# A fused attention and two-MLP kernel on one core: places for activations in the first MLP's blocks, the pace of the second weights' conversions, and places for the last splits

## The chip, the cores and the metric

The kernel runs on one core of one Trainium2 chip. The metric is device time in microseconds (us), the median of several runs. Before the change it is 1630.62 us, the median of 3 runs (1630.06 to 1632.49).

## The reference

```python
def _attn_ref(q, k, v, g_norm):            # 8 batches, 8 heads, 576 tokens, 64 wide
    kv = np.einsum('bhsd,bhse->bhde', k, v)
    out = np.einsum('bhsd,bhde->bhse', q, kv)
    rms = np.sqrt(np.mean(out * out, axis=-1, keepdims=True) + 1e-06)
    return out / rms * g_norm
def _moe_ref(x, w_in, w_out, s, b):        # x 4608 x 512, w_in 512 x 2048, w_out 2048 x 512
    r = np.maximum(x @ w_in, 0.0)
    return (s * (r * r) + b) @ w_out
def _moe2_ref(x, w_in, w_out):
    h = x @ w_in
    return (h * np.cos(h)) @ w_out
# reference: attention, then x as 4608 x 512, then _moe_ref, then _moe2_ref, all float32;
# the weights arrive as float64
```

## The kernel before, in words

The work has three stages. **Stage A** does the attention and the first MLP for three blocks of 512 tokens. **Stage B** does the first MLP for the other tokens, in four blocks of 768, as 32 pairs (a pair is two of the sixteen 128-wide slices of the 2048 hidden columns; 90 matmuls). **Stage C** does the second MLP for all tokens, in six blocks of 768, as 48 pairs. Stages B and C form the first matmul of a pair from seven products of sums of quarters (`mm_h2`, line 966, matmuls at L981); each product leaves a bank of PSUM by a copy on ACT, the "snap" (L994), or by a sum on DVE (L1001 in stage B, L1003 in stage C). The second matmul is `mm_o1` in stage B (L875) and seven "units" per pair in stage C (`mm_unit`, L1092), three at once and four stored ones, which are worked off a block later. Fp32 operands go to the PE as an upper and a lower part: the upper is a cast on ACT, the lower a subtraction on DVE (L1203 and L1204 in stage B, in `act1_pair`; L1029 and L1030 in stage C, in `split_form`).

During stage B the weights of the second MLP are also made ready (`w_conv`): a load of 512 KB into the single place `raw` (L388, L392), then ACT (L405, L415) and DVE (L406 to L423), then sums and splits (`w_sums`, `o_sums`, `split_store`; L456, L458, L477, L504) whose parts go to DRAM (`w2i_d`, `w2n_d`, `w2s_d`; L467, L495). The five places `t0` to `t4` hold both those parts, until their store has landed, and the snaps.

The order of the work on every engine is not written by hand: `Plan.run` simulates all engines with the costs given to `op`, and issues each operation when its model would start it; among those ready, the one with the earliest `due`. Each engine then works in that order, and waits on the chip for what is really late. A DMA is assumed to land `LANDS` = 0.5 us after its transfer. Buffers are named places; an operation takes the place that comes free first in the model. The places that matter:

```python
RING, PLACES, X_RAW = WI[:6], slots("s", 11), LATE[:4]   # weights of stage B; raw x
RING2, O_RING, ACTS2 = WI[:5], WI[5:9], WI[9:]           # stage C: weights, activations
NOW, STORED = [*SPLIT_F[3:], *RAW], SPLIT_F[:3]          # splits of units
ACTS1 = WI[6:]                                           # activations of stage B
```

`WI` has sixteen places `wi0` to `wi15`. In stage B a pair takes six of `ACTS1`: two for h, two for upper and two for lower parts. At the very end `block_out` works off 32 stored units of the last block (four sums `y0` to `y3`, the loop over p, of eight units each); between them DVE adds each finished sum to what is kept (L1136).

Of the kernel before, what the change touches and what calls it, by code (L numbers as in the profile page):

```python
# [12 lines left out]
F32R = mybir.dt.float32r  # L13
# [9 lines left out]
TB2 = 768  # L23
# [22 lines left out]
NOW_AT = tuple(UNIT_STEP * i for i in (2, 5, 8))  # L46
STORED_AT = 10 * UNIT_STEP
FIRST_LOADS = {0: -39.5, 1: -38.5, 2: -36.5, 3: -36.3}
WARM = 24
# [22 lines left out]
class Plan:  # L72
# [18 lines left out]

    def op(self, eng, cost, due, fn, w=(), p=(), r=(), keep=(), after=()):

        o = Op()
        o.eng, o.cost, o.due, o.fn, o.refs = eng, cost, due, fn, list(dict.fromkeys([*w, *p, *r, *keep]))
        deps = set(after)
        for x in r:
            deps.update(x.writers)  # L100
        for x in w:
            deps.update(x.writers)
            deps.update(x.readers)
        for x in p:
            deps.update(x.readers)
        for x in r:
            x.readers.append(o)
        for x in w:
            x.writers, x.readers = [o], []
        for x in p:  # L110
            x.writers.append(o)
        deps.discard(o)
        o.wait, o.users, o.ready = len(deps), [], 0.0
        for d in deps:
            d.users.append(o)
        for x in o.refs:
            x.left += 1
        self.ops.append(o)
        return o

    def run(self):
# [31 lines left out]
        while n < len(self.ops):  # L153
# [13 lines left out]
            if o.eng in self.ISSUE:  # L167
                engines[o.eng] = t + self.ISSUE[o.eng]
                dma = max(dma, t + self.TO_DMA) + o.cost * self.BUSY
                end = seen = dma + self.LANDS  # L170
                lanes[o.eng].pop(0)
                lanes[o.eng].append(end)
            else:
                end = engines[o.eng] = t + o.cost * self.SLACK[o.eng]
                seen = end + self.AFTER[o.eng]
# [20 lines left out]
def fused_kernel(  # L196
# [126 lines left out]

    RING, PLACES, X_RAW = WI[:6], slots("s", 11), LATE[:4]
    RING2, O_RING, ACTS2 = WI[:5], WI[5:9], WI[9:]
# [5 lines left out]
    ACTS = PARTS = [*WI[6:], *RAW]  # L331
    ACTS1 = WI[6:]
    SNAP = [*T, *C]
# [44 lines left out]
    def w_conv(ph, kind, f, by, load_by=None, after=()):  # L378
# [23 lines left out]

        op("SP", 1.45 if kind == "i" else 1.35, by - 12 if load_by is None else load_by, load, w=[raw], after=after)

# [47 lines left out]
    def split_store(t, n, by, ref, to, start=0):  # L452
# [9 lines left out]
        for z, part in enumerate((hi, lo)):  # L462
# [5 lines left out]

            op("SP", n * 0.0013, by, store, p=[ref], r=[part])

    def o_sums(u, tu, tv, by):
# [19 lines left out]
        for t, parts in ((ya, ((now[:, 2], w2n_ref[u]), stored(2))), (yb, (stored(1), stored(3)))):  # L491
            both = split_store(t, 512, by, None, None)
            for z, part in enumerate(both):
                for n, (d, ref) in enumerate(parts):
                    op("SP", 0.335, by, lambda z=z, part=part, n=n, d=d: nc.sync.dma_start(  # L495
                        out=d[:, z, :], in_=f32(part.t[:, n * HB:(n + 1) * HB])), p=[ref], r=[part])

# [619 lines left out]
    def block_out(j):  # L1117
# [32 lines left out]
        for p in range(4):  # L1150
            name = f"y{p}" if end else "y"
            for u in range(NU):
# [3 lines left out]
                f = stored_f[n0 + u][p]  # L1156
                x = split_form(STORED, lambda f=f: f.t, f, at - 3)
                after = []
# [36 lines left out]
    def act1_pair(n, h):  # L1195

        g = {}
        for f, by in ((1, pair_due(n + 1)), (0, pair_due(n + 1) + 2)):
            x, hi, lo = h[f], *(sref(ACTS1, F32R, (TB2,)) for z in range(2))
            op("ACT", 0.75, by, lambda x=x: nc.scalar.activation(x.t, x.t, AF.Square), w=[x])  # L1200
# [3 lines left out]
            op("DVE", 0.88, by + 5, lambda x=x, hi=hi, lo=lo: nc.vector.tensor_tensor(  # L1204
                out=lo.t, in0=x.t, in1=f32(hi.t), op=ALU.subtract), w=[lo], r=[x, hi])
            g[f] = lambda z, hi=hi, lo=lo: (hi, lo)[z].t, [hi, lo]
# [59 lines left out]
    for n in range(NPAIR):  # L1266
# [8 lines left out]
        while n and n < NP1 and done_convs < 4 * NU and (  # L1275
                done_convs - EARLY_CONVS) * (NP1 - 10) <= (n - 1) * (4 * NU - EARLY_CONVS):
            conv2(pair_due(n + 1) + 24, [done[n - 1]])
# [50 lines left out]
```

## Time and profile before

| | |
|---|---|
| median of 3 runs | 1630.62 us |
| the profiled execution, its own time | 1630.51 us |
| its span, first to last instruction | 1628.7 us |
| PE busy | 1596.6 us (98%), 11248 matmuls |
| DVE busy / ACT busy | 1150.5 us (71%) / 1124.9 us (69%) |
| DMA | 383.71 MB, mean 236 GB/s |

The profiled execution takes 1.8 us outside its span. Stage A runs to about 361 us, stage B to about 899 us, stage C to the end. The engines work side by side, so the time is set by PE, which has nearly all the work, and by what PE waits for.

### The profile page before, as it was taken

To read this page: it belongs to the slowest core of one execution; us is meant where nothing else is said; L and a number is where in the kernel's file an instruction comes from. 1 tells how busy PE (TensorE), PEld (TensorE's weight loads), DVE (VectorE), ACT (ScalarE), POOL (GpSimd) and SP (SyncE) were. 2 spreads that over 40 slices of the span, in tenths; PEclk is the share of its full clock that TensorE was granted. 3 is DMA by queue.
4 is the path that set the end of the run, shared out by engine and by line. 5 is a ranking of instruction groups with operands and counts; after the bars stand their busy time and mean duration, and the time that the engine had idled before them with its cause. 6 is when DMAs were issued, how large, how long until landed. Compare 5 with 4: busy or idle time off the path is not lost.

```text
span 1628.7 us, 30373 instructions
## 1 busy us (share of the span) xinstructions
PE 1596.6 (98%) x11248; PEld 1468.8 (90%) x11248; DVE 1150.5 (71%) x2194; ACT 1124.9 (69%) x2013; POOL 54.5 (3%) x90
## 2 busy tenths in 40 slices
PE   8999999999999999999999899999999999999998
PEld 7668888889898998899999889999999999999997
DVE  6887775674655665657323798887888888888775
ACT  5865543446576676667545898788788788788773
POOL 0011222100000000000000000000000000000000
PEclk9999999999999999999999999999999999999999
DMA  9746878847678878878644777878878878878866
GB/s 317 224 105 170 219 194 202 259 120 234 219 235 278 281 232 267 280 231 267 200 130 135 224 236 232 303 245 269 302 237 267 306 249 272 298 256 258 270 205 196
DMA packets 240180, 383.71 MB, mean 236 GB/s; under 512 B 86432, under 2 KB 152480, under 8 KB 240032
## 3 DMA queue, kind: packets, MB, share of 16 engines
q1 hardware_dynamic: 233440, 360.20, 70.2%
q0 software_dynamic: 6016, 20.45, 4.6%
q8 instruction: 89, 1.46, 0.4%
q10 hardware_dynamic: 576, 1.11, 0.2%
q14 instruction: 59, 0.48, 0.1%
HBM read 312.48 MB, written 69.21 MB: 234 GB/s over the span
## 4 chain that ended last, share of the span: by engine, by line
PE 87%; DMA 5%; ACT 4%; DVE 3%; issue 1%; SPq 0%; POOL 0%; DVEq 0%; ACTq 0%; POOLq 0%
PE banks L981 31%; PE banks L1092 20%; PE banks L875 13%; PE banks L827 6%; PE banks L774 3%; PE banks L775 3%; PE banks L776 3%; PE banks L823 3%; PE banks L600 1%; PE banks L694 1%; DMA raw<-in_moe_w_in_dram 1%; PE banks L732 1%; DMA w2i_d<-t 1%; DMA w2n_d<-t 1%; DMA w2s_d<-t 1%
## 5 line engine op out<-in xcount | busy, mean ns | idle before, releaser
L981 PE MATMUL banks<-shared,wi 128*128 128x384 f32 x2232 | 455.7, 338 | 9.8 <-ACT t L994 7.1
L981 PEld LDWEIGHTS banks<-shared,wi 128*128 128x128 f32 x2232 | 388.0, 188 | 19.1 <-ACT t L994 10.5
L1092 PE MATMUL banks<-wi,fs 128*128 128x256 f32 x2376 | 309.0, 283 | 4.7 <-DVE fs L1030 3.0
L1092 PEld LDWEIGHTS banks<-wi,fs 128*128 128x128 f32 x2376 | 301.6, 190 | 6.9 <-DVE fs L1030 4.5
L875 PE MATMUL banks<-wi,wo 128*128 128x512 f32 (+1 forms) x1536 | 290.3, 337 | 3.0 <-DVE wi L1204 3.0
L875 PEld LDWEIGHTS banks<-wi,wo 128*128 128x128 f32 x1536 | 244.7, 188 | 34.0 <-DVE wi L1204 5.5
L994 ACT ACTIVATE t<-banks 128x384 f32<-128x384 f32 x214 | 104.1, 488 | 90.7 <-PE banks L981 67.3
L1030 DVE TENSOR_TENSOR fs<-fu,fs 128x384 fp32r<-128x384 f32 x216 | 116.4, 553 | 31.7 <-ACT fs L1029 30.6
L1029 ACT CAST fs<-fu 128x384 fp32r<-128x384 f32 x216 | 108.4, 507 | 35.2 <-PE banks L1092 34.9
L981 PE MATMUL banks<-late,wi 128*128 128x384 f32 x552 | 116.7, 338 | 2.1 <-DVE wi L1001 1.5
L981 PE MATMUL banks<-g,wi 128*128 128x384 f32 x504 | 113.4, 340 | 2.6 <-ACT t L994 1.6
L827 PE MATMUL banks<-g,wo 128*128 128x512 f32 x432 | 108.9, 395 | 0.0
L1204 DVE TENSOR_TENSOR wi<-wi,wi 128x768 fp32r<-128x768 f32 x64 | 59.6, 954 | 62.9 <-PE banks L875 61.8
L981 PEld LDWEIGHTS banks<-late,wi 128*128 128x128 f32 x552 | 95.3, 188 | 4.6 <-DVE wi L1001 2.1
L1049 DVE CUSTOM_DVE_ANT_0 wi<-wi,wi 128x768 f32<-128x768 f32 x96 | 91.3, 952 | 7.3 <-ACT wi L1047 7.0
L827 PEld LDWEIGHTS banks<-g,wo 128*128 128x128 f32 x432 | 79.7, 188 | 17.2
L1043 ACT ACTIVATE wi<-wi 128x768 f32<-128x768 f32 x96 | 80.2, 842 | 16.2 <-DVE wi L1003 14.6
L981 PEld LDWEIGHTS banks<-g,wi 128*128 128x128 f32 x504 | 85.6, 188 | 5.3 <-ACT t L994 2.8
L1092 PE MATMUL banks<-wi,raw 128*128 128x256 f32 x648 | 89.8, 283 | 0.4 <-DVE raw L1030 0.3
L1092 PEld LDWEIGHTS banks<-wi,raw 128*128 128x128 f32 x648 | 85.9, 189 | 1.4 <-DVE raw L1030 1.0
L774 PE MATMUL banks<-shared,wi 128*128 128x512 f32 x192 | 82.2, 428 | 1.9 <-ACT shared L751 1.6
L1045 ACT ACTIVATE wi<-wi 128x768 f32<-128x768 f32 x96 | 80.7, 841 | 2.7 <-PE banks L875 1.2
(171 smaller groups left out, 2439.8 us busy)
## 6 DMA issues: line engine op xcount, KB each, us to landing
wi<-w2i_d SPq DMA_DIRECT2D x144, 512.0 KB, 4.7
wi<-w1i_d SPq DMA_DIRECT2D x96, 512.0 KB, 4.8
wi<-w2s_d SPq DMA_DIRECT2D x96, 512.0 KB, 4.5
wi<-w2n_d SPq DMA_DIRECT2D x48, 512.0 KB, 4.3
late<-x_d SPq DMA_DIRECT2D x36, 384.0 KB, 6.5
w2i_d<-t SPq DMA_DIRECT2D x48, 256.0 KB, 4.4
wi<-w2n_d SPq DMA_DIRECT2D x48, 256.0 KB, 4.1
wi<-w2i_d SPq DMA_DIRECT2D x48, 256.0 KB, 4.5
```

Source lines behind the costliest of these rows:

```text
L774: nc.tensor.matmul(h.t, wh, hi, start=(c == 0), stop=False)
L827: nc.tensor.matmul(o.t, a[:, sl], b, start=(first and z == 0), stop=(last and z == 2))
L875: nc.tensor.matmul(dst, x[:, sl], y[:, src], start=(first and z == i == 0), stop=(last and z == 2), skip_group_check=a >= 4)
L981: nc.tensor.matmul(o.t[:, 0:HT], a, b, start=(first and c == z == 0), stop=(c == 1 and z == 2), skip_group_check=not first)
L994: op("ACT", 0.38, by + 1, lambda: nc.scalar.activation(dst(), o.t[:, 0:HT], func), p=[s], r=[o])
L1029: op("ACT", 0.42, by, lambda: nc.scalar.copy(x.t[:, 0], src()), w=[x], r=[ref], after=after)
L1030: op("DVE", 0.47, by + 0.4, lambda: nc.vector.tensor_tensor(out=x.t[:, 1], in0=src(), in1=f32(x.t[:, 0]), op=ALU.subtract), w=[x], r=[ref])
L1043: op("ACT", 0.75, by, lambda u=u, x=x: nc.scalar.activation(u.t, x.t, AF.Identity, scale=1.0 / TWO_PI, bias=0.25), w=[u], r=[x])
L1045: op("ACT", 0.75, by + 0.5, lambda u=u, v=v: nc.scalar.activation(v.t, u.t, AF.Identity, bias=MAGIC), w=[v], r=[u])
L1049: op("DVE", 0.88, by + 2, lambda u=u, v=v: nc.vector._custom_dve(TENSOR_ADD_SAT, out=u.t, in0=u.t, in1=v.t, s0=0.5 - 1.7e-7, s1=-0.5 + 1.7 ...
L1092: nc.tensor.matmul(dst, x.t[:, a, sl], w.t[:, at, b, :], stop=(last and z == 2), start=(first and z == 0 and (m == 0 or (m == 2 and opens) ...
L1204: op("DVE", 0.88, by + 5, lambda x=x, hi=hi, lo=lo: nc.vector.tensor_tensor(out=lo.t, in0=x.t, in1=f32(hi.t), op=ALU.subtract), w=[lo], r= ...
```

## The change

1. `op` gets a `lag`, which `run` adds to the time at which it assumes a DMA has landed: 2.5 us for the loads of the second weights (`w_conv` with ph = 1), 1.5 us for the stores of their parts (and for those of stage A that go through `split_store`).
2. The ring of stage B's weights has five places instead of six; the sixth, `wi5`, goes to the activations (eleven instead of ten).
3. The lower parts of stage B's activations may also lie in the four places of raw x (`LOWER`); they wait until those places exist (`after=over`).
4. The 32 conversions are spread over stage B to its 27th pair or so, instead of its 22nd (`NP1 - 5` for `NP1 - 10`).
5. In the last block the splits of the sums `y1` to `y3` may also lie in the seven places `ACTS2`, once the units done at once (a, b, c) are through.

```diff
+LOAD_LAG, STORE_LAG = 2.5, 1.5
...
-                end = seen = dma + self.LANDS
+                end = seen = dma + self.LANDS + o.lag
...
-    RING, PLACES, X_RAW = WI[:6], slots("s", 11), LATE[:4]
+    RING, PLACES, X_RAW = WI[:5], slots("s", 11), LATE[:4]
...
-    ACTS1 = WI[6:]
+    ACTS1 = WI[5:]
+    LOWER = [*ACTS1, *X_RAW]
...
-        op("SP", 1.45 if kind == "i" else 1.35, by - 12 if load_by is None else load_by, load, w=[raw], after=after)
+        op("SP", 1.45 if kind == "i" else 1.35, by - 12 if load_by is None else load_by, load, w=[raw], after=after,
+           lag=LOAD_LAG if ph else 0.0)
...
-            op("SP", n * 0.0013, by, store, p=[ref], r=[part])
+            op("SP", n * 0.0013, by, store, p=[ref], r=[part], lag=STORE_LAG)
...
-                x = split_form(STORED, lambda f=f: f.t, f, at - 3)
+                free = end and p
+                x = split_form([*STORED, *ACTS2] if free else STORED, lambda f=f: f.t, f, at - 3,
+                               [unit_ops[j, z, "last"] for z in "abc"] if free else ())
...
-            x, hi, lo = h[f], *(sref(ACTS1, F32R, (TB2,)) for z in range(2))
+            x, hi, lo = h[f], *(sref(s, F32R, (TB2,)) for s in (ACTS1, LOWER))
...
-                out=lo.t, in0=x.t, in1=f32(hi.t), op=ALU.subtract), w=[lo], r=[x, hi])
+                out=lo.t, in0=x.t, in1=f32(hi.t), op=ALU.subtract), w=[lo], r=[x, hi], after=over)
...
-                done_convs - EARLY_CONVS) * (NP1 - 10) <= (n - 1) * (4 * NU - EARLY_CONVS):
+                done_convs - EARLY_CONVS) * (NP1 - 5) <= (n - 1) * (4 * NU - EARLY_CONVS):
```

No operation is added or removed; what changes is places and, through the model, the order on each engine. Lines behind the edits have moved by one to six: L1204 becomes L1210, L1030 L1034, L1136 L1140. Three places show what moves.

DVE in stage B, two lower parts of the 17th pair (L1204; after the change L1210). A name is a place's kind and a running number; a row's brackets hold the engines it waits for. Before:

```order
L458 TENSOR_TENSOR t_7006<-c_6976,t_7005 128x512 [waits DMAHW5_49,DMAHW7_49,DMAHW2_49,Activation_49]
L1204 TENSOR_TENSOR wi_7034<-wi_6896,wi_6943 128x768 [waits PE_49]
L1204 TENSOR_TENSOR wi_7038<-wi_6818,wi_6991 128x768
L406 TENSOR_SCALAR c_7036<-c_7036 128x512 [waits Activation_49]
L408 TENSOR_SCALAR c_7036<-c_7036 128x512 [waits DVE_49]
```

and with the change:

```order
L461 TENSOR_TENSOR t_6824<-c_6804,t_6823 128x512 [waits DMAHW1_49,Activation_49]
L890 COPY t_6855<-banks 128x512 [waits PE_49]
L1210 TENSOR_TENSOR late_6861<-wi_6785,wi_6850 128x768 [waits Activation_49]
L1210 TENSOR_TENSOR late_6877<-wi_6741,wi_6863 128x768 [waits Activation_49]
L409 TENSOR_SCALAR c_6874<-c_6874 128x512 [waits Activation_49]
```

The two now lie in places of raw x (`late`) and no longer wait for PE. Over stage B's 64 lower parts, 38 waited for PE before and 20 do now; 30 lie in `late`, and one of those waits for PE.

ACT at the start of stage C: the first pair's chain of cosine steps (L1043, L1045, L1047, then L1051 with its table load; after the change L1047, L1049, L1051, L1055), the last block's evacuations of stage B (L888, now L892) and snaps (L994, now L998). Before:

```order
L1043 ACTIVATE wi_9357<-wi_9297 128x768 [waits DVE_49,Activation_49]
L888 COPY t_9388<-banks 128x512 [waits PE_49]
L888 COPY t_9403<-banks 128x512 [waits PE_49]
L994 ACTIVATE c_9413<-banks 128x384 [waits PE_49]
L1043 ACTIVATE wi_9431<-wi_9362 128x768 [waits DVE_49,PE_49]
L994 ACTIVATE c_9439<-banks 128x384 [waits PE_49]
L994 ACTIVATE c_9447<-banks 128x384 [waits PE_49]
L994 ACTIVATE c_9464<-banks 128x384 [waits PE_49]
L1045 ACTIVATE wi_9485<-wi_9431 128x768 [waits PE_49,Activation_49]
```

and with the change:

```order
L1047 ACTIVATE wi_9351<-wi_9337 128x768 [waits DVE_49,Activation_49]
L1049 ACTIVATE wi_9359<-wi_9351 128x768 [waits PE_49,Activation_49]
L998 ACTIVATE wi_9293<-banks 128x384 [waits PE_49]
L1051 ACTIVATE wi_9359<-wi_9359 128x768 [waits Activation_49]
L1047 ACTIVATE wi_9374<-wi_9293 128x768 [waits Activation_49]
L1049 ACTIVATE wi_9386<-wi_9374 128x768 [waits DVE_49,Activation_49]
L1055 ACT_TABLE_LOAD
L1055 ACTIVATE wi_9351<-wi_9351 128x768
L892 COPY t_9398<-banks 128x512 [waits DMAHW6_49,DMAHW5_49,PE_49]
L1051 ACTIVATE wi_9386<-wi_9386 128x768 [waits Activation_49]
L892 COPY t_9414<-banks 128x512 [waits DMAHW2_49,DMAHW1_49,PE_49]
L998 ACTIVATE c_9423<-banks 128x384 [waits PE_49]
```

The chain with its table load has moved ahead of the evacuations and of the next pair's snaps; before, the table load stood six rows below the last row shown.

DVE in the last block, around the adds behind the sum `y0` (L1136, now L1140) and the lower parts of the stored units (L1030, now L1034; `fs` are the three places `STORED`). Before:

```order
L1030 TENSOR_TENSOR fs_18211<-fu_16804,fs_18211 128x384 [waits Activation_49]
L1030 TENSOR_TENSOR fs_18225<-fu_16977,fs_18225 128x384 [waits Activation_49]
L1136 TENSOR_TENSOR c_18098<-banks,c_18098 128x512 [waits DMAHW1_49,DMAHW0_49,Activation_49]
L1136 TENSOR_TENSOR fe_18102<-banks,fe_18102 128x256 [waits DMAHW7_49,Activation_49]
L1136 TENSOR_TENSOR t_18172<-banks,t_18172 128x512
L1136 TENSOR_TENSOR c_18174<-banks,c_18174 128x256
L1136 TENSOR_TENSOR c_18115<-banks,c_18115 128x512
L1136 TENSOR_TENSOR t_18118<-banks,t_18118 128x256
L1030 TENSOR_TENSOR fs_18245<-fu_17144,fs_18245 128x384 [waits PE_49,Activation_49]
```

and with the change:

```order
L1034 TENSOR_TENSOR wi_18170<-fu_16804,wi_18170 128x384 [waits Activation_49]
L1034 TENSOR_TENSOR wi_18176<-fu_16977,wi_18176 128x384 [waits Activation_49]
L1034 TENSOR_TENSOR fs_18194<-fu_17865,fs_18194 128x384 [waits Activation_49]
L1034 TENSOR_TENSOR wi_18189<-fu_17144,wi_18189 128x384
L1034 TENSOR_TENSOR fs_18209<-fu_18047,fs_18209 128x384 [waits Activation_49]
L1034 TENSOR_TENSOR wi_18197<-fu_17326,wi_18197 128x384
L1034 TENSOR_TENSOR wi_18212<-fu_17513,wi_18212 128x384 [waits Activation_49]
L1034 TENSOR_TENSOR wi_18226<-fu_17695,wi_18226 128x384 [waits Activation_49]
L1140 TENSOR_TENSOR c_18098<-banks,c_18098 128x512 [waits DMAHW1_49,DMAHW0_49,Activation_49]
```

Two splits of `y1` stood ahead of the adds; six do now, in `wi` places. Ahead of the next adds stand all eight of `y2`.

## Rows read from the trace of the kernel before

**Rows 1.** Busy time by stretch (stage B, start of stage C, last block); columns as headed.

```profile
core 0: us, PE busy (x) PEld busy (x) DVE busy (x) ACT busy (x) POOL busy (x), PEclk, DMA share, GB/s
361.00:899.00 538.00, 529.10 (x2987) 489.09 (x2986) 289.82 (x526) 340.99 (x562) 0.00 (x0) 1.00 0.72 228
899.00:1000.00 101.00, 92.82 (x568) 86.72 (x567) 87.32 (x165) 90.77 (x158) 0.00 (x0) 1.00 0.71 231
...
1575.00:1628.70 53.70, 45.65 (x356) 44.25 (x355) 33.10 (x66) 22.31 (x47) 0.00 (x0) 0.97 0.67 209
```

**Rows 2.** Waits of PE in stage B: engine, line, releaser: us in total, times, longest.

```profile
PE banks L981 <- ACT t L994: 4.1, 8, 0.8
PE banks L875 <- DVE wi L1204: 3.0, 4, 0.8
PE banks L981 <- DVE wi L1001: 1.5, 1, 1.5
```

**Rows 3.** Timeline of PE around one gap: start, us, operation, [idle before, releaser].

```profile
635.46 0.88 PE L875 MATMUL banks<-wi,wo 128*128 128x256 f32 x6
636.18 1.21 PE L981 MATMUL banks<-g,wi 128*128 128x384 f32 x6
637.23 1.11 PE L875 MATMUL banks<-wi,wo 128*128 128x256 f32 x7
639.15 0.73 PE L875 MATMUL banks<-wi,wo 128*128 128x512 f32 x2 [0.82 <-DVE wi L1204]
```

**Rows 4.** Waits of DVE and of ACT in stage B.

```profile
DVE wi L1204 <- PE banks L875: 61.8, 26, 5.2
ACT c L405 <- DMA raw<-in_moe_w_in_dram: 25.3, 12, 4.0
```

**Rows 5.** Chain that ended last, stage B: two DMAs on it (start, us).

```profile
645.45 6.80 DMA raw<-in_moe_w_in_dram
...
678.31 7.96 DMA w2n_d<-t
```

**Rows 6.** DMA issues: count, KB each, median us from issue to landing.

```profile
wi<-w1i_d SPq DMA_DIRECT2D x96, 512.0 KB, 4.8
...
raw<-in_moe_w_in_dram SPq DMA_DIRECT2D x16, 512.0 KB, 5.5
...
w2s_d<-t SPq DMA_DIRECT2D x64, 128.0 KB, 4.1
```

**Rows 7.** Busy time before and after the start of stage C.

```profile
884.00:898.00 14.00, 14.00 (x80) 13.05 (x80) 4.43 (x7) 5.26 (x9) 0.00 (x0) 1.00 0.55 184
898.00:1000.00 102.00, 93.82 (x575) 87.72 (x574) 87.53 (x165) 91.12 (x158) 0.00 (x0) 1.00 0.72 230
```

**Rows 8.** Timeline of ACT, and of PE (last row), there.

```profile
898.65 0.85 ACT L1045 ACTIVATE wi<-wi 128x768 f32<-128x768 f32 x1 [1.22 <-PE banks L875]
...
902.61 1.28 ACT L1051 ACT_TABLE_LOAD   x1
...
906.32 1.33 PE L981 MATMUL banks<-shared,wi 128*128 128x384 f32 x6 [2.79 <-ACT t L994]
```

**Rows 9.** Waits of PE in the last block, and DVE's timeline there.

```profile
PE banks L1092 <- DVE fs L1030: 3.0, 2, 1.7
PE banks L1092 <- DMA wi<-w2s_d: 0.7, 2, 0.6
...
1593.45 0.69 DVE L1136 TENSOR_TENSOR c<-banks,c 128x512 f32<-128x512 f32 x1 [0.23 <-ACT t L1169]
...
1596.25 1.48 DVE L1030 TENSOR_TENSOR fs<-fu,fs 128x384 fp32r<-128x384 f32 x3
```

**Rows 10.** The stretch in which the granted clock fell, and the next.

```profile
1608.00:1611.40 3.40, 3.40 (x18) 3.40 (x18) 0.90 (x2) 1.01 (x2) 0.00 (x0) 0.51 0.28 102
1611.40:1617.50 6.10, 6.10 (x53) 6.10 (x53) 4.22 (x9) 2.58 (x6) 0.00 (x0) 1.00 0.66 206
```

**Rows 11.** A wait of SP's queue in stage B.

```profile
SPq L467 <- ACT t L456: 34.6, 21, 4.2
```

More of the change, by code (lines that the diff above doesn't have):

```diff
@@ L90, in __init__, with op @@
         self.parts = {}
-    def op(self, eng, cost, due, fn, w=(), p=(), r=(), keep=(), after=()):
+    def op(self, eng, cost, due, fn, w=(), p=(), r=(), keep=(), after=(), lag=0.0):
         o = Op()
-        o.eng, o.cost, o.due, o.fn, o.refs = eng, cost, due, fn, list(dict.fromkeys([*w, *p, *r, *keep]))
+        o.eng, o.cost, o.due, o.fn, o.lag, o.refs = eng, cost, due, fn, lag, list(dict.fromkeys([*w, *p, *r, *keep]))
         deps = set(after)
@@ L495, in o_sums @@
                     op("SP", 0.335, by, lambda z=z, part=part, n=n, d=d: nc.sync.dma_start(
-                        out=d[:, z, :], in_=f32(part.t[:, n * HB:(n + 1) * HB])), p=[ref], r=[part])
+                        out=d[:, z, :], in_=f32(part.t[:, n * HB:(n + 1) * HB])), p=[ref], r=[part],
+                       lag=STORE_LAG)
     def w_sums(u, tu, tv, by, whole_ones=True):
```

## The prediction

> **What bounds the kernel now.** I read the busy times by stretch first. PE is the bound everywhere: in stage B it is busy 529.1 of 538.0 us, at the start of stage C 92.8 of 101.0, in the last block 45.7 of 53.7 [rows 1]. No matmul is added or taken away, so the time can only change by the idle time of PE, and by its clock. The idle times to be had are 8.9 us in stage B, 8.2 at the start of stage C and 8.0 in the last block; of the last, the end behind PE's last matmul stays.
>
> Second, the waits of PE say what ends its idle time. In stage B it is no DMA of its own but ACT and DVE being late: eight gaps behind snaps (4.1 us), four behind lower parts (3.0), one behind a sum (1.5) [rows 2]. Those 8.6 us are not all that the gaps cost. In the timeline six 256-wide matmuls take 0.72 us from their start to the next group's start (636.18 less 635.46), so seven take 0.84, but the seven before the gap take 1.92 (639.15 less 637.23) [rows 3]. The gap is shown with 0.82 and costs 1.08: each costs 0.26 us more than shown. Stage B's 13 gaps cost 8.6 + 13 x 0.26 = 12.0 us.
>
> Third, why ACT and DVE are late although they are idle for a third of stage B and more. DVE waits 61.8 us at L1204 for PE: the place of a lower part is still being read [rows 4]. ACT waits 25.3 us for raw loads of the second weights [rows 4], with snaps queued behind. Two pieces of the chain that ended last show the same: a raw load of 6.80 us and a store of 7.96 us, for whose place a snap waited [rows 5]. The planner takes about 3.8 us for a raw load (1.4 + 1.45 x 1.3 + 0.5, its constants); the trace has a median of 5.5 [rows 6].
>
> **The change part by part.** (a) Places for lower parts. All four gaps behind L1204 cost 3.0 + 4 x 0.26 = 4.0 us. In the new order two of these four pairs no longer wait for PE at all, the 17th among them (shown), and over the stage 20 of 64 lower parts wait where 38 did. I take half: -2.0. Bounds: nothing, and -4.0.
>
> (b) The lags. With 2.5 us more the planner assumes 6.3 us for a raw load, above the median of 5.5 [rows 6]; for a 256 KB store it assumes 1.4 + 0.67 x 1.3 + 0.5 + 1.5 = 4.3, for a 128 KB store 3.8, beside a median of 4.1 for the latter [rows 6]. So ACT should be given other work until a transfer has landed. The nine gaps behind snaps and the sum, 5.6 + 9 x 0.26 = 7.9 us, go back mostly to such transfers. Those of median length are covered now; the long ones are not (6.80 and 7.96 us [rows 5]). I take half: -4.0. Bounds: nothing, and -7.9. The Trainium skill (DMA: Bandwidth & Descriptors, "Latency and other measured facts") gives HBM latency as 0.2 us on average and 2 us at high load. By that rule a constant allowance fails just where DMAs crowd, and (b) would be near 0; the trace shows the spread, with no cause.
>
> (c) Conversions over some 27 pairs instead of 22: the same work, less of it per pair. It has no gap of its own; it supports (b). It runs into pairs where ACT has room: between 884 and 898 us ACT is busy 5.26 of 14 [rows 7]. Nothing.
>
> (d) New waits. An order made for later landings puts some PE work elsewhere, and the ring of weights has one place less. I allow two gaps of middle size (0.5 + 0.26 each, from rows 2): +1.5 us, between 0 and +4. Stage A is reordered in a few places through the store lag; PE has full cover there and I take 0. Together stage B gives -2.0 - 4.0 + 1.5 = -4.5 us.
>
> (e) Start of stage C. ACT is the tightest there: 91.1 of 102 us from 898, with 8.7 us idle in the 14 us before [rows 7]. L1045 stood waiting for PE to release a place, the table load (1.28 us) came after it, and a snap behind these cost PE its longest gap, 2.79 [rows 8]. Lower parts in raw x places free those places, and in the new order the first pair's chain with the table load comes before the evacuations: some 4 us of ACT work (the table load and three or four operations of 0.85) move into idle time. The gap itself is worth 2.79 + 0.26 = 3.05; of the rest of this stretch's 8.2 us I take a backlog of 1.5 less. -4.5 us. Bounds: -8.2, and +3 if a snap now waits behind the chain in front of it (one more gap of the longest kind).
>
> (f) Last block. PE waits twice for lower parts, 3.0 us [rows 9], 3.5 with 0.26 each. The cause is plain: behind a finished sum DVE does its adds from 1593.45 to 1596.25 and only then the next split [rows 9], with only three places for splits. In the new order six splits of the next sum stand ready in `wi` places; at 9 x 0.12 = 1.1 us each they cover the 2.8 us of adds. So -3.5. Bounds: -3.5, and -1.7 if one remains.
>
> (g) The clock. Right behind the second of these gaps the granted clock is 0.51 for 3.4 us (1.2 GHz instead of 2.4): 18 matmuls start there, while the next stretch has 53 in 6.10, 0.115 us each [rows 10]. The dip costs 3.4 - 18 x 0.115 = 1.3 us. The stretch before it is the one with the two gaps; without them I expect no dip: -1.3. Bounds: 0 and -1.3. The longer gap of 2.79 us at 906 [rows 8] was followed by no dip. The Trainium skill (TensorE: Matmul & The Clock Gate, "What's actually happening") has the clock released by activity and throttled after idleness; by that rule the dip would go too, but the gap at 906 shows that not every gap has one.
>
> **The sum.** -4.5 - 4.5 - 3.5 - 1.3 = -13.8 us. The profiled execution took 1630.51 us, 0.11 under the median of the runs, so 1630.5 - 13.8 = 1616.7, and 1616.8 as a median. What can be told from no change here is about 0.2%, 3.3 us.
>
> **The rivals.**
> - R1, stage B's gaps only move: terms (a), (b) and (d) sum to 0, because the long transfers set them and a planner cannot foresee these. For it: the two transfers of rows 5; the table of waits shows many causes. Against it: 18 waits for places are gone from the order. Time: 1630.6 - 9.3 = 1621.3. The rule on latency under load named in (b) leads here.
> - R2, only the last block gains: R1, and ACT remains the bound at the start of stage C (87.5 and 91.1 of 102 us busy on DVE and ACT [rows 7]), so that (e) is 0. Time: 1630.6 - 4.8 = 1625.8.
> - R3, everything goes: all 12.0 us of stage B, 8.2 of stage C's start, 4.8 at the end: 1605.6 at best.
> - R4, no change: the chain in front of the snaps costs (e) +3 instead of -4.5, stage B 0, and in the last block the weights' loads take over as the bound, which PE already waits for (0.7 us in two gaps [rows 9]), so that half of (f) and (g) is lost. About 1630.6 + 3 - 2.4 = 1631.2.
> - R5, slower: the ring of five. SP's queue is worked in order, and a weight load that stands behind a store waits with it. The tightest tile of the ring comes free some 6.7 us into a pair (five products of 1.05, 637.23 less 636.18, and two groups of 0.72 between them [rows 3]) and the next is needed 3.9 us into the following pair (three products and one group); a pair takes 90 x 538 / 2987 = 16.2 us [rows 1], so there are 13.4 us for a load of 4.8 [rows 6], 8.6 us to spare. It decides only where SP is held longer than that. The longest hold by anything but PE is 4.2 us [rows 11]. To undo 13.8 us and lose 3.3 more, the 32 pairs would have to wait 0.5 us each. Time: 1634 or more.
>
> **How the numbers follow.** My forecast, -8 to -20 us, 0.57; R1 0.18; R2 0.08; R3 0.07; R4 0.05; R5 0.05. Likeliest 1616.8. The range takes in the forecast, R1 and R2: 1608 (stage B -10, (e) -8, end -4.8) to 1626.5; R3's far end, R4 and R5 are left out. Faster 0.57 + 0.18 + 0.08 + 0.07 = 0.90; same 0.05; slower 0.05.
>
> **What would show it.** In the profile after, PE's waits of the last block should have no lower part left and the clock should be 1.00 there (f, g); in stage B ACT's waits for raw loads should fall from 25.3 us to under 10 and DVE's for PE at the lower parts from 61.8 to about half (a, b); the table load should lie before 898 us or in ACT's idle time, and the 2.8 us gap be gone (e). I am wrong if PE waits for `w1i_d` loads (R5), if its gaps in stage B have the same sum with other releasers (R1), or if the first 100 us of stage C still show 8 us of idle PE (R2).

## The result, and the profile after

The kernel takes 1610.33 us (median of 4 runs, 1609.47 to 1613.54) where the one before took 1630.34 us in the same comparison: ratio 0.9879, 95% interval 0.9862 to 0.9896, so some 20 us faster. The direction was right and the time lies in the range, but the forecast of 1616.8 us had 13.8 us of gain where there are about 20. The profiled execution took 1611.06 us, its span is 1609.2 us, and PE is busy for 1589.4 us of it (99%).

To see where the time went I took the starts of the same matmuls in both traces. The first product of stage C (33rd pair) is one of them; the timeline of PE shows it in the kernel before

```profile
874.22 0.70 PE L981 MATMUL banks<-g,wi 128*128 128x384 f32 x3
```

and in the changed kernel, where the line is L985:

```profile
863.98 0.69 PE L985 MATMUL banks<-late,wi 128*128 128x384 f32 x3
```

That is 10.24 us earlier. With the fifth pair's first product, the last product and the last matmul as further marks, the change against before is:

| stretch | after minus before | forecast |
|---|---|---|
| to the fifth pair of stage B | -0.2 us | 0 |
| from there to stage C's first product | -10.0 us | -4.5 (a, b, d) |
| stage C to its last product | -4.1 us | -4.5 (e) |
| the rest | -5.2 us | -4.8 (f, g) |
| sum | -19.5 us | -13.8 |

So stage B gave twice what I forecast, and the two other places about what I forecast (these are single profiles; the last section shows one pair of the same order that differs by 2.8 us in stage B). The busy times by stretch, in the columns of [rows 1]; the last block ends 19.5 us earlier, so its stretch is moved, and the fourth row is a stretch inside the second:

```profile
361.00:899.00 538.00, 535.11 (x3051) 498.95 (x3049) 305.01 (x547) 353.86 (x586) 0.00 (x0) 1.00 0.74 233
...
899.00:1000.00 101.00, 94.57 (x589) 90.59 (x589) 85.41 (x162) 86.30 (x154) 0.00 (x0) 0.98 0.74 236
1555.50:1609.20 53.70, 48.75 (x400) 47.91 (x398) 35.58 (x71) 26.45 (x55) 0.00 (x0) 1.00 0.74 228
957.90:961.30 3.40, 3.40 (x13) 3.40 (x11) 3.35 (x8) 2.70 (x6) 0.00 (x0) 0.51 0.09 34
```

PE's idle time falls from 8.9 to 2.9 us in the first stretch, from 8.0 to 5.0 in the last block, and only from 8.2 to 6.4 at the start of stage C (moved ten us earlier like the work, to 889 to 990, it is 6.6), where a dip of the clock has come in that the profile of before does not have there (the last row: 13 matmuls in 3.4 us, granted clock 0.51, 1.2 GHz instead of 2.4).

The waits of PE in 361 to 899 are now two gaps, where [rows 2] had 13:

```profile
PE banks L985 <- ACT t L998: 1.9, 1, 1.9
PE banks L879 <- DVE wi L1210: 0.8, 1, 0.8
```

Of ACT's and DVE's waits there, these bear on the change (compare [rows 4]; the `late` line is that of the lower parts in raw x places):

```profile
ACT c L408 <- DMA raw<-in_moe_w_in_dram: 0.5, 1, 0.5
...
DVE wi L1210 <- ACT wi L1209: 20.8, 11, 4.4
DVE wi L1210 <- PE banks L879: 18.9, 6, 5.2
...
DVE late L1210 <- ACT wi L1209: 13.5, 11, 2.6
```

ACT's waits for raw loads of `w_in` fell from 25.3 to 0.5 us, and the lower parts' waits for PE from 61.8 to 18.9; for most of the time that they wait now (34.3 us), they wait for the cast on ACT that they need.

The longer of the two gaps left goes back to a single store; on the chain that ended last it stands as

```profile
590.44 8.71 DMA w2i_d<-t
```

At the start of stage C the longest gap of [rows 8] is gone; in the last block of the changed kernel only a gap of 0.54 us behind a weight load is left. PE's timeline, rows with idle time ahead, from the start of stage C and, the last row, from the last block:

```profile
919.42 0.79 PE L985 MATMUL banks<-late,wi 128*128 128x384 f32 x3 [1.30 <-ACT t L998]
...
922.57 0.79 PE L985 MATMUL banks<-late,wi 128*128 128x384 f32 x3 [0.78 <-ACT c L998]
...
957.25 1.70 PE L985 MATMUL banks<-shared,wi 128*128 128x384 f32 x6 [1.17 <-DVE wi L1007]
...
1571.12 1.30 PE L1096 MATMUL banks<-wi,fs 128*128 128x256 f32 x9 [0.54 <-DMA wi<-w2s_d]
```

And ACT's timeline has the table load 13.6 us behind stage C's first product (877.54 less 863.98) where it stood 28.4 behind it (902.61 less 874.22):

```profile
877.54 1.28 ACT L1055 ACT_TABLE_LOAD   x1
```

### The profile page after: what moved, and what is told of

It reads as the page before. It is cut to its first block, busy times and chain, and to the rows that moved or that the text cites. A ratio compares the mean times of both kernels' runs of the same rounds, so it can differ in the third digit from the quotient of the medians.

```text
span 1609.2 us, 30384 instructions
## 1 busy us (share of the span) xinstructions
PE 1589.4 (99%) x11248; PEld 1468.8 (91%) x11248; DVE 1155.5 (72%) x2194; ACT 1121.6 (70%) x2013; POOL 54.5 (3%) x90
## 4 chain that ended last, share of the span: by engine, by line
PE 94%; ACT 2%; DMA 2%; DVE 1%; issue 0%; POOL 0%; DVEq 0%; SPq 0%; POOLq 0%; ACTq 0%
PE banks L985 35%; PE banks L1096 21%; PE banks L879 16%; PE banks L831 6%; PE banks L778 3%; PE banks L780 3%; PE banks L779 3%; PE banks L827 3%; PE banks L604 1%; PE banks L698 1%; PE banks L736 1%; DMA w2i_d<-t 1%; PE banks L1221 0%; DMA late<-x_d 0%; DMA kv_raw<-in_v_dram 0%
## 5 line engine op out<-in xcount | busy, mean ns | idle before, releaser
L985 PE MATMUL banks<-shared,wi 128*128 128x384 f32 x2232 | 467.4, 338 | 2.9 <-ACT t L998 1.6
L985 PEld LDWEIGHTS banks<-shared,wi 128*128 128x128 f32 x2232 | 390.7, 188 | 8.2 <-ACT t L998 2.9
L1096 PE MATMUL banks<-wi,fs 128*128 128x256 f32 x2214 | 287.8, 283 | 1.0 <-DMA wi<-w2s_d 0.5
L1096 PEld LDWEIGHTS banks<-wi,fs 128*128 128x128 f32 x2214 | 280.9, 190 | 2.5 <-issue 1.0
L879 PE MATMUL banks<-wi,wo 128*128 128x256 f32 (+1 forms) x1296 | 281.0, 337 | 0.8 <-DVE wi L1210 0.8
L879 PEld LDWEIGHTS banks<-wi,wo 128*128 128x128 f32 x1296 | 213.7, 188 | 25.8 <-DVE wi L1210 1.6
L998 ACT ACTIVATE t<-banks 128x384 f32<-128x384 f32 x218 | 105.9, 488 | 119.0 <-PE banks L985 86.9
L985 PE MATMUL banks<-late,wi 128*128 128x384 f32 x552 | 126.2, 341 | 3.0 <-ACT t L998 2.3
L1034 DVE TENSOR_TENSOR fs<-fu,fs 128x384 fp32r<-128x384 f32 x198 | 106.3, 555 | 20.2 <-ACT fs L1033 19.2
L985 PE MATMUL banks<-g,wi 128*128 128x384 f32 x504 | 116.4, 339 | 2.2 <-ACT t L998 2.2
L1033 ACT CAST fs<-fu 128x384 fp32r<-128x384 f32 x198 | 99.1, 506 | 17.8 <-PE banks L1096 17.6
L985 PEld LDWEIGHTS banks<-late,wi 128*128 128x128 f32 x552 | 96.3, 190 | 6.2 <-ACT t L998 3.2
L1053 DVE CUSTOM_DVE_ANT_0 wi<-wi,wi 128x768 f32<-128x768 f32 x96 | 91.6, 954 | 11.6 <-ACT wi L1051 11.3
L831 PEld LDWEIGHTS banks<-g,wo 128*128 128x128 f32 x432 | 79.7, 188 | 17.1
L1047 ACT ACTIVATE wi<-wi 128x768 f32<-128x768 f32 x96 | 80.4, 841 | 15.0 <-DVE wi L1007 14.6
L985 PEld LDWEIGHTS banks<-g,wi 128*128 128x128 f32 x504 | 86.2, 188 | 4.1 <-ACT t L998 3.1
L792 ACT ACTIVATE t<-banks 128x512 f32<-128x512 f32 x48 | 28.6, 596 | 77.0 <-PE banks L780 75.1
L1055 ACT ACTIVATE wi<-wi 128x768 f32<-128x768 f32 x96 | 80.6, 840 | 1.2 <-DVE wi L1053 0.9
```

Of the source, the lines that this page charges most:

```text
L831: nc.tensor.matmul(o.t, a[:, sl], b, start=(first and z == 0), stop=(last and z == 2))
L879: nc.tensor.matmul(dst, x[:, sl], y[:, src], start=(first and z == i == 0), stop=(last and z == 2), skip_group_check=a >= 4)
L985: nc.tensor.matmul(o.t[:, 0:HT], a, b, start=(first and c == z == 0), stop=(c == 1 and z == 2), skip_group_check=not first)
L998: op("ACT", 0.38, by + 1, lambda: nc.scalar.activation(dst(), o.t[:, 0:HT], func), p=[s], r=[o])
L1033: op("ACT", 0.42, by, lambda: nc.scalar.copy(x.t[:, 0], src()), w=[x], r=[ref], after=after)
L1034: op("DVE", 0.47, by + 0.4, lambda: nc.vector.tensor_tensor(out=x.t[:, 1], in0=src(), in1=f32(x.t[:, 0]), op=ALU.subtract), w=[x], r=[ref])
```

## The experiments

Two theories stood against each other for stage B. **Lags**: the gaps come from transfers that land later than planned, so edit 1 carries the stage (my term b). **Places**: the gaps come from places that come free late, so edits 2 and 3 carry it (term a). Gains "in us" below are the ratio's, on 1630.3 us. In each diff `+` is the kernel that ran, and `...` marks lines left out.

### One edit at a time, on the kernel before

**e1_ends: edit 5 alone.**

```diff
-                x = split_form(STORED, lambda f=f: f.t, f, at - 3)
+                free = end and p
+                x = split_form([*STORED, *ACTS2] if free else STORED, lambda f=f: f.t, f, at - 3,
+                               [unit_ops[j, z, "last"] for z in "abc"] if free else ())
```

> The kernel before with edit 5 alone (last splits also in ACTS2). Both theories: stages A, B and the start of stage C as before (gaps in stage B 8.6 us by the waits of PE, ACT waiting 25.3 us for raw loads); PE waits for no lower part in the last block, no fall of the granted clock; 5 us faster, 1625.4, between 1624.5 and 1626.5. If the loads of the last weights took over as the bound, no more than 2.5 us faster.

1626.19 us, ratio 0.9976 (0.9966 to 0.9986): 3.9 us. Behind the last product the profile gains 5.0 us, and in the last block PE waits for a weight load alone. The instruction order on every engine is that of before up to the last block; yet this one profile is 2.8 us ahead at stage C's first product. So stage B differs by that much between two executions of one order, and the medians decide below where single profiles only point.

**e2_lags: edit 1 alone.**

```diff
+LOAD_LAG, STORE_LAG = 2.5, 1.5
...
-                end = seen = dma + self.LANDS
+                end = seen = dma + self.LANDS + o.lag
...
```

> The kernel before with edit 1 alone (lags of 2.5 and 1.5 us in the planner's landings). Theory L (stage B lost its time to transfers that the planner assumed too early): stage B's gaps fall from 8.6 us to under 3, ACT's waits for raw loads from 25.3 to under 10 us, 8 us faster, about 1622. Theory P (it lost it to places for lower parts): the gaps behind L1204 stay, 3 us faster at most, 1627 or more.

1626.78 us, ratio 0.9984 (0.9975 to 0.9994): 2.6 us. Waits in 361 to 899, of PE and of ACT:

```profile
PE banks L984 <- ACT t L997: 4.1, 5, 1.6
PE banks L878 <- DVE wi L1207: 2.9, 4, 0.8
PE banks L984 <- DVE wi L1004: 0.5, 1, 0.5
...
ACT c L407 <- DMA raw<-in_moe_w_in_dram: 1.6, 1, 1.6
```

The lags do exactly what they are for: 25.3 us of waits for raw loads become 1.6. And PE still stands for 7.5 us of its 8.6 [rows 2]: 2.9 behind lower parts, as before, and 4.6 instead of 5.6 behind snaps and the sum. I followed each of these gaps back through whatever released it last. In the kernel before, six of the nine gaps behind snaps and the sum, 4.3 of the 5.6 us, lead to a load or a store of the second weights. Here two of six do, 1.3 us; three others, 2.9 us, lead to stores and loads of x, which get no lag. ACT's timeline has the waits for x in front of two of them:

```profile
761.73 0.49 ACT L997 ACTIVATE t<-banks 128x384 f32<-128x384 f32 x1 [1.54 <-DMA x_d<-t]
...
806.72 0.51 ACT L936 CAST shared<-late 128x384 fp32r<-128x384 f32 x1 [2.09 <-DMA late<-x_d]
```

**e3_places: edits 2 and 3 alone.**

```diff
-    RING, PLACES, X_RAW = WI[:6], slots("s", 11), LATE[:4]
+    RING, PLACES, X_RAW = WI[:5], slots("s", 11), LATE[:4]
...
-    ACTS1 = WI[6:]
+    ACTS1 = WI[5:]
+    LOWER = [*ACTS1, *X_RAW]
...
-            x, hi, lo = h[f], *(sref(ACTS1, F32R, (TB2,)) for z in range(2))
+            x, hi, lo = h[f], *(sref(s, F32R, (TB2,)) for s in (ACTS1, LOWER))
...
```

> The kernel before with edits 2 and 3 alone (eleventh place, lower parts also in places of raw x, ring of five). Theory P: the gaps in stage B fall from 8.6 us to under 3 and stage C starts earlier, 8 to 10 us faster, 1620 to 1622. Theory L: ACT still waits some 25 us for raw loads, the four gaps behind lower parts go but those behind snaps stay, 2 to 5 us faster, 1625 to 1628.

1619.49 us, ratio 0.9932 (0.9917 to 0.9947): 11.1 us, the largest piece by far. Between the marks it is 4.8 us in stage B and 4.1 in stage C. The waits of PE and DVE in stage B:

```profile
PE banks L982 <- ACT t L995: 5.7, 5, 1.9
PE banks L876 <- DVE wi L1205: 0.7, 1, 0.7
...
DVE wi L1205 <- PE banks L876: 16.3, 7, 5.1
```

PE's waits for lower parts are nearly gone, those for snaps are longer than before. Followed back, all five gaps behind snaps lead to transfers of the second weights, which get no lag here: four to stores, one to a raw load. Three of ACT's waits in front of them:

```profile
443.82 0.49 ACT L995 ACTIVATE t<-banks 128x384 f32<-128x384 f32 x1 [3.91 <-DMA w2s_d<-t]
...
584.84 0.66 ACT L406 ACTIVATE c<-raw 128x512 f32<-128x512 f32 x1 [3.89 <-DMA raw<-in_moe_w_in_dram]
...
717.32 1.13 ACT L995 ACTIVATE t<-banks 128x384 f32<-128x384 f32 x2 [2.17 <-DMA w2i_d<-t]
```

The time is what theory P expected and more; the gaps are what theory L did. So each edit removes the gaps that it names, and gaps of other kinds stay or come in their place. ACT's waits for raw loads of `w_in` are 6.6 us here, without any lag: that they fell does not by itself show the lags at work.

**e4_conv: edit 4 alone.**

```diff
-                done_convs - EARLY_CONVS) * (NP1 - 10) <= (n - 1) * (4 * NU - EARLY_CONVS):
+                done_convs - EARLY_CONVS) * (NP1 - 5) <= (n - 1) * (4 * NU - EARLY_CONVS):
```

> The kernel before with edit 4 alone (conversions over some 27 pairs). Both theories: the same waits, spread over five more pairs; stage B's gaps between 6 and 9 us, 0 to 2 us faster, 1628.5 to 1630.6. A third theory (C: it is the density of ACT's and DVE's work per pair that makes them late): gaps under 4 us and 6 us faster, 1624.5.

1631.12 us, ratio 1.0003 (0.9992 to 1.0013): nothing, as (c) had it.

The single edits sum to 17.1 us against 19.7 together; the difference of 2.6 lies within the intervals (4.7 by the root of the sum of their squares), so these four runs alone do not show that the edits help each other.

### One edit taken out of the change

**f1_nolags.**

```diff
-LOAD_LAG, STORE_LAG = 2.5, 1.5
+LOAD_LAG, STORE_LAG = 0.0, 0.0
```

> The changed kernel with both lags set to zero; all else as in the change. If the buffer places carry stage B and the lags do nothing but move ACT's waits, 1610 to 1612 us (the lags alone gave 3, within their interval of 1 to 4), with ScalarE's waits for raw back above 8 us while TensorE's waits in 361 to 899 stay under 5. If the lags carry it, as the prediction's largest stage B term had it, 1615 or more and the snap waits back at 6 or more.

1617.9 us, ratio 0.9929 (0.9914 to 0.9943): without the lags 8.1 us of the gain are lost. The snap gaps are back, the lower parts' are not:

```profile
PE banks L985 <- ACT t L998: 4.9, 7, 1.4
PE banks L985 <- DVE wi L1005: 0.8, 1, 0.8
PE banks L879 <- DVE wi L1210: 0.7, 1, 0.7
...
ACT c L408 <- DMA raw<-in_moe_w_out_dram: 16.8, 8, 4.0
...
ACT t L998 <- DMA w2i_d<-t: 9.6, 7, 2.1
```

**f2_noplaces.** Edits 2 and 3 of the change taken back, the rest kept.

```diff
-    RING, PLACES, X_RAW = WI[:5], slots("s", 11), LATE[:4]
+    RING, PLACES, X_RAW = WI[:6], slots("s", 11), LATE[:4]
...
-    ACTS1 = WI[5:]
-    LOWER = [*ACTS1, *X_RAW]
+    ACTS1 = WI[6:]
...
```

> The changed kernel without the eleventh place and without the raw x places for lower parts; lags, later conversions and last splits kept. Adding up the single edits gives 1610.3 + 11 = 1621 us (1619 to 1624), the gaps for snaps and lower parts in 361 to 899 back at 6 to 8, and the start of the next stage again some 4 later. If lags and places only work together, 1624 or more; if each can stand in for the other, 1616 or less.

1625.92 us, ratio 0.9971 (0.9961 to 0.9981): 15.0 us of the gain are lost, more than the sum of single edits would have it. The gaps have swapped sides:

```profile
PE banks L878 <- DVE wi L1209: 6.4, 8, 0.8
PE banks L984 <- ACT t L997: 2.0, 3, 0.9
```

Counting gains with edit 5 in all four (e1, f2, f1 and the change; edit 4, which is worth nothing alone and nothing beside all the others, is in the last three):

| gain in us | without places | with places |
|---|---|---|
| without lags | 3.9 | 11.6 |
| with lags | 4.7 | 19.7 |

The lags are worth 0.8 us without the places and 8.1 with them; the places 7.7 without the lags and 15.0 with them. Each entry is uncertain by 1.6 to 2.8 us (half its interval), the difference of 7.3 by the root of the sum of their squares, 4.3; it is there, its size is rough. Two things make it rougher: edit 4 beside the places without the lags was not measured apart, and e3, the places alone, gained 11.1 us where the table has 7.7. The starts of the same matmuls say the same of stage B: the five profiles with both lags and places gain 7.7 to 11.9 us there (the change, f3, g1, g2, h1), the four with one of the two 1.7 to 4.8 (e2, e3, f1, f2), and e1 and e4, with neither, 2.8 and 1.9. Neither theory holds alone: there are two obstacles, and time is gained in full only where both are gone.

**f3_noconv.** Edit 4 taken out.

```diff
-                done_convs - EARLY_CONVS) * (NP1 - 5) <= (n - 1) * (4 * NU - EARLY_CONVS):
+                done_convs - EARLY_CONVS) * (NP1 - 10) <= (n - 1) * (4 * NU - EARLY_CONVS):
```

> The changed kernel with the second weights' conversions at the old pace. Alone this edit did nothing (1631.1 against 1630.0). If it does nothing beside the places either, 1610.3 within 1.5. If the freed places let it spread work off the first units of the third stage, 1613 to 1616, with the waits for snaps in 899 to 1000 longer by 3 or more.

1612.01 us, ratio 0.9888 (0.9872 to 0.9905). That cannot be told from the change's 0.9879: the later conversions are worth nothing here either.

**f4_nolower.** Edit 2 without edit 3: eleven places, lower parts held to them.

```diff
-    LOWER = [*ACTS1, *X_RAW]
...
-            x, hi, lo = h[f], *(sref(s, F32R, (TB2,)) for s in (ACTS1, LOWER))
+            x, hi, lo = h[f], *(sref(ACTS1, F32R, (TB2,)) for z in range(2))
...
```

> The changed kernel with the eleventh place for activations and the ring of five, but lower parts held to those eleven, so no raw x place is used. If the one added place does the work, 1610 to 1613 us with VectorE's lower parts waiting for TensorE 15 to 25 us in all. If the raw x places do the work, 1617 to 1621, the lower parts waiting over 35 us and TensorE's gaps before pair products back at 6 or more.

1621.86 us, ratio 0.9948 (0.9933 to 0.9962). The raw x places are worth 11.2 us of the change (19.7 less 8.5), the eleventh place 3.8 (8.5 less f2's 4.7). DVE's waits in stage B:

```profile
DVE wi L1209 <- PE banks L878: 51.4, 20, 5.2
```

and PE's timeline at the start of stage C:

```profile
903.17 0.79 PE L984 MATMUL banks<-late,wi 128*128 128x384 f32 x3 [2.80 <-ACT c L997]
```

Without the raw x places the lower parts wait nearly as long as before, and the longest gap of [rows 8] is still there, with the eleventh place alone: between stage C's first and last product f4 gains 0.1 us, the change 4.1.

### How far the knobs go

**g1_ring4.** A ring of four places for stage B's weights (the expectation's words name it wrongly; it is the ring `RING`, which holds the first MLP's), twelve for activations.

```diff
-    RING, PLACES, X_RAW = WI[:5], slots("s", 11), LATE[:4]
+    RING, PLACES, X_RAW = WI[:4], slots("s", 11), LATE[:4]
...
-    ACTS1 = WI[5:]
+    ACTS1 = WI[4:]
```

> The changed kernel with one more step in the same direction: second weights' ring of four places, twelve for activations. This is the prediction's slower rival put to the test one place further. If a ring of four still covers a landing of 4.6 us, 1608 to 1611 us and no wait of TensorE for w1i or w2 loads. If loads become late, TensorE waits for a ring load in most of the pairs, and at 0.5 us or more for each of some 36 pairs the time is 1628 or more.

1608.56 us, ratio 0.9865 (0.985 to 0.9879). No wait of PE is for a load into `RING`, and its waits in 361 to 899 are:

```profile
PE banks L879 <- DVE wi L1210: 0.8, 1, 0.8
PE banks L985 <- ACT t L998: 0.2, 1, 0.2
PE banks L985 <- ACT wi L998: 0.2, 1, 0.2
```

The slower rival falls with a margin: one place fewer still costs nothing that shows. This is the fastest median of the study, but its interval overlaps the change's, so it is not shown to be better.

**g2_lags2.** Both lags doubled.

```diff
-LOAD_LAG, STORE_LAG = 2.5, 1.5
+LOAD_LAG, STORE_LAG = 5.0, 3.0
```

> The changed kernel with both lags doubled, 5.0 and 3.0. If the lags help by putting the dependent work late enough, and 2.5 and 1.5 already cover the landings of 4.4 and 4.5 us, nothing is left: 1609 to 1612. If landings over the median still cost, 1606 to 1609 and no wait of ScalarE for raw at all. If lags also displace other work, as any order change can, 1613 or more with snap waits back in 361 to 899.

1617.73 us, ratio 0.9919 (0.9904 to 0.9933): 6.5 us slower than the change. ACT has no wait for raw loads left in stage B, so there was little more to earn from these, and each of the three later stretches is worse: 7.7 us gained in stage B instead of 10.0, 2.3 instead of 4.1 and 3.6 instead of 5.2. The waits for snaps in 361 to 899 did not come back, though (2.2 us against 1.9), so the expectation of displaced work has the time and not its sign, and what the larger lags displace is not shown. Over the whole span PE waits twice for second weights, among others:

```profile
PE banks L985 <- ACT t L998: 5.6, 8, 1.9
...
PE banks L1096 <- DMA wi<-w2s_d: 2.1, 2, 1.2
PE banks L879 <- DVE wi L1210: 1.6, 2, 0.9
```

**g3_load.** The lag on raw loads alone.

```diff
-LOAD_LAG, STORE_LAG = 2.5, 1.5
+LOAD_LAG, STORE_LAG = 2.5, 0.0
```

> The changed kernel with the lag on raw loads alone, none on stores. With both at zero it was 1617.9, with both 1610.3. If the raw loads carry the 7.6, 1610 to 1612; if the stores do, whose source places t are what TensorE's snaps go into, 1615 to 1618 and longer waits of ScalarE for the stores w2i_d, w2n_d, w2s_d.

1615.4 us, ratio 0.9905 (0.9888 to 0.9921): between the two. Of the lags' 8.1 us the loads' gives 3.9 over f1 and the stores' the other 4.2; each is about as large as its own uncertainty. ACT's snaps wait for one kind of store more than twice as long as with both lags:

```profile
ACT t L998 <- DMA w2i_d<-t: 14.1, 8, 3.2
```

(6.6 us in 4 waits in the changed kernel.) For the three kinds of stores of the second weights together they wait 24.6 us, against 15.4 with both lags and 15.6 with none, so the sum of these waits does not order the three times.

**h1_ring4_xlag.** g1, and a lag of 2.5 us on the raw x loads.

```diff
...
+               lag=2.5 if j else 0.0)
```

> Ring of four places as in g1 (1608.6), and the lag of 2.5 also on the loads of raw x, which land in 6.5 us and one of which, from 912.59 to 919.39, stands in the chain of waits ahead of the 1.30 us gap at 919.42. If that load is what the first units of the third stage lack, the gaps in 899 to 1000 shrink from 6 to 3 and the time is 1605 to 1607. If a longer planned landing only moves other work, as the doubled lags did (7 us slower), 1610 to 1616, with the gain of the second stage, 11.9 at the start of the third, smaller.

1610.92 us, ratio 0.9876 (0.9859 to 0.9892): no gain over the change or g1. Its named gap is gone; PE's waits in 899 to 1000 are

```profile
PE banks L986 <- ACT t L999: 1.9, 3, 1.4
PE banks L986 <- DVE wi L1008: 1.2, 1, 1.2
```

and 0.8 us in three short ones, 3.9 in all. Between stage C's first and last product it gains 6.9 us over before where g1 gains 4.1, and in stage B it gives 3.5 of g1's back (8.4 against 11.9). Stage B's figures vary by some 3 us between executions, so that this loss comes from the new order is likely and not shown.

## Why the prediction was right or wrong

**Right: what bounds the kernel, the start of stage C, the last block.** No matmul changed and the time came out of PE's idle time. The signs named for it came: raw waits under 10 us (e3 has that one without the lags, so it could not tell (b) from (a)), lower parts' waits under half, the table load earlier, no lower part and no dip in the last block. (e) was -4.5 and the trace has -4.1, with the mechanism as put: with lower parts in raw x places the chain and its table load come earlier (877.54), and the 2.79 us gap goes; f4 shows that it takes these places. The gain was held down by a dip of the clock that had not been there: f1 and f3, with the same places and no dip, gain 5.4 and 5.2 us in that stretch. (f) was -3.5: behind the last product the profiles with edit 5 gain 4.6 to 5.7 us (g2's 3.6 apart) and those without it 0.9 to 1.8; the difference, 2.8 to 4.8, holds the 3.5.

**Right in mechanism, too small in size: (b).** The nine gaps do go back mostly to transfers of the second weights, as the term has it: six of them, 4.3 of 5.6 us (in two of the six ACT stood for under 0.2 us, so there the transfer is a small part of the lateness); in e1, which has the same order, 3.5 of 3.9 us. Four of ACT's waits in front of them, in the kernel before:

```profile
459.41 0.49 ACT L994 ACTIVATE t<-banks 128x384 f32<-128x384 f32 x1 [1.87 <-DMA w2s_d<-t]
493.58 0.66 ACT L405 ACTIVATE c<-raw 128x512 f32<-128x512 f32 x1 [2.30 <-DMA raw<-in_moe_w_in_dram]
...
652.27 0.66 ACT L405 ACTIVATE c<-raw 128x512 f32<-128x512 f32 x1 [2.15 <-DMA raw<-in_moe_w_in_dram]
...
721.64 1.10 ACT L994 ACTIVATE t<-banks 128x384 f32<-128x384 f32 x2 [1.47 <-DMA w2i_d<-t]
```

With places and without lags all the gaps behind snaps are of this kind in e3 (5.7 us), and 3.5 of the 5.7 us behind snaps and the sum in f1; with both, one is left in the change (1.9 us), none in f3 and g1, and one or two where lags were moved further (g2, h1). The step that failed is "I take half: -4.0", as if the long transfers had to stay: beside the places nearly all of it goes. What the term missed is that it does not go alone. e2 cut the gaps of its kind from 4.3 to 1.3 us, and gaps behind transfers of x (0.25 us before, 2.9 in e2) took most of that back. The rule weighed there, that HBM latency rises tenfold under load (the Trainium skill, DMA: Bandwidth & Descriptors, "Latency and other measured facts"), would have had a constant allowance fail. On the whole it did not fail: beside the places it is worth 8.1 us, raw waits of 25.3 us became 0.5, and doubling the constant earned nothing. The rule's case remains in one gap, behind the store that took 8.71 us.

**Right in mechanism, too small in size: (a).** I priced the places by the four gaps that name L1204, at 2.0 us and at most 4.0. e3 has 4.8 us in stage B alone. In company it is more, because the number of such gaps is not fixed: f2, with the lags and without the places, has eight of them (6.4 us) where the change has one (0.8), and gains 1.7 us in stage B where the change gains 10.0. e2 has four; in stage B the two differ by edit 4 alone, so the number hangs on the order. The rest of the 15.0 us that the places are worth in company lies in stage C (f2 2.0 us behind before, the change 4.1 ahead), which is term (e). The gaps with other names were not theirs: followed back, none of the nine in the kernel before passes a lower part's wait.

**Wrong in form: the sum.** I added (a) and (b), half of each, and 1.5 us of new waits. In full and with no new waits they would be 4.0 + 7.9 = 11.9 us; the five profiles with lags and places have 7.7 to 11.9. Taken singly, the gaps that one remedy removes are partly replaced, so neither part has a worth of its own that could simply be halved and summed: lags 0.8 us without places and 8.1 with. That is also where R1 was half right: with one remedy alone PE's waits in 361 to 899 stay near what they were, in other places (7.5 us in e2, 8.4 in f2, 6.4 in e3 and in f1, of 8.6). Both together leave 2.7. Rival R3's stage B, -12.0, was nearer (-10.0) than my -4.5.

**(d)** was right in kind: the one long gap left, 1.9 us at 599.77, is a new one. **(c)** at nothing held, alone and in company.

**(g): the time was there, the reason not.** In the last block of e2, e3 and e4 PE waits 3.0 us for the same two lower parts as before [rows 9], and no dip follows: e2's granted clock in that block is 0.99 and that of the two others 1.00, against 0.97 [rows 1]. The 0.9 to 1.8 us that these three gain there without edit 5 fit the 1.3 us that I put on the dip. So the price was right for the profile of before, but the dip does not belong to those gaps, and the sum should have had it at less than 1.3 us. The change has one in another place. The rule named there (the Trainium skill, TensorE: Matmul & The Clock Gate, "What's actually happening": activity releases the throttle, idleness brings it back) names idleness; here the same two gaps were followed by a dip in one profile and not in three, and these runs do not show which gap brings one.

**R5** was rightly given little: PE waits for no load into `RING` with five places or with four. [rows 11] covers a part of stage B only: over 361 to 899 that wait is 41.3 us in 26 times, and the longest hold by anything but PE is 5.0 us instead of 4.2, still under the 8.6 to spare.

## What to carry to other kernels

When a list orders work by planned landings and a pool of places, try the two remedies together as well as apart: one alone can look nearly worthless (here the lags, 0.8 to 2.6 us) because other gaps take the place of those that it removes. Before pricing a wait of a helper engine, ask whether the bound engine's gap goes back to it, and then remove that wait and see whether the time comes back or another gap takes its place. Here the constant that helped at the size of a real landing cost 6.5 us when it was doubled, so set it from the landing measured and test before going further.

## What the runs showed that I had not expected

**The clock dips behind the same gap in one execution and not in another.** Before stage C's first units are through, the gap of 2.79 to 2.81 us occurs in before, e1, e2, e4, f2 and f4. The granted clock falls right behind it in e1, e2, e4 and f2, but not in before and f4. The stretch behind it in e1, in the columns of [rows 1]:

```profile
904.50:907.90 3.40, 3.40 (x16) 3.40 (x16) 3.24 (x7) 3.08 (x6) 0.00 (x0) 0.54 0.00 0
```

In before, the stretch behind that gap has 22 matmuls at a clock of 1.00:

```profile
906.30:909.70 3.40, 3.38 (x22) 3.38 (x23) 3.24 (x8) 3.10 (x6) 0.00 (x0) 1.00 0.01 5
```

A later gap behind L1003 (or the line it has become), 1.17 to 1.19 us long in all fourteen profiles, has a dip behind it in the changed kernel, e3, e4, g1 and h1, and none in the nine others. So a forecast can give such a dip a chance, not a place. It also moves the medians a little: over the 56 executions of the kernel before that are on record with their clock, the mean granted clock was 0.996 to 1.000, and those at 0.997 took 1631.8 us on average where those at 1.000 took 1629.0; the changed kernel's four are all at 0.999 or 1.000. An estimate from these figures is that some 1 us of the 20 is clock and not PE's waits.

**One order, stage B 2.8 us apart.** e1 and before have the same instructions in the same order on every engine up to the last block, and differ by 2.8 us at stage C's first product, with no dip of the clock in either between the first 10 us and that point. Whoever reads a gain of 3 us in one stage from one profile may be reading noise.
